# Second half of the next pair's y loaded at the 19th unit of the passes, not the 24th, into other rooms

## The chip, the cores and the metric

One core of a Trainium2 chip runs the whole program. The metric is device time in microseconds, as the median of several runs. Five engines work side by side, each in the order of its own instructions: TensorE (PE in the profile; PEld is its weight load), VectorE (DVE), ScalarE (ACT), GpSimd (POOL) and SyncE (SP), which here issues most DMA transfers. 16 DMA engines move the data; SP's transfers are queue q1 in the profile, GpSimd's are q0.

## The reference

```python
def _attn_ref(q, k, v, mem_k, mem_v):          # chunks of 32 queries, 16 + 32 + 8 keys and 8 memory keys
    ...
        scores = scale * np.matmul(q_c, k_full.transpose(0, 1, 3, 2))
        a = np.exp(scores - np.max(scores, axis=-1, keepdims=True))
        out[:, :, c_start:c_end] = np.matmul(a / (np.sum(a, axis=-1, keepdims=True) + 1e-09), v_full)

def _moe_ref(x, w_in, w_out):
    h = x @ w_in
    return (np.maximum(h, 0.0) + np.log1p(np.exp(-np.abs(h)))) @ w_out

def _moe2_ref(x, w_in, w_out, alpha):
    h = x @ w_in
    return (np.maximum(h, 0.0) + alpha * np.minimum(h, 0.0)) @ w_out

x = attn_out.transpose(0, 2, 1, 3).reshape(B * S, H * D)      # 3072 tokens x 512
return _moe2_ref(_moe_ref(x, ...), ...)                       # 512 -> 2048 -> 512, twice; all float32
```

## The kernel before, in words

Attention and the first MLP fill the first part of the program, under an order that a planner in the kernel works out; the change touches nothing of it. Their result y, 512 rows by 3072 tokens, lies in device memory (`y_dram`), in six blocks of 512 tokens.

The second MLP takes the blocks in three pairs, p = 0, 1, 2. For a pair it multiplies 2x2 blocked matrices with seven products in place of eight (Winograd's form of Strassen's method), so that it works on sums and differences of blocks. Each float32 operand is split in a high and a low part, and each product is three matmuls. A pair has two stages of 336 matmuls:

- **Quads** (`quad`, eight of them): x operands (`xop`) times `win`. The results G[0] to G[3] lie in tiles `gb`.
- **Passes** (`second`): seven passes of eight *units*, n = 0 to 55. A unit takes one G tile, splits it into a `g` tile (a cast on ScalarE for the high part, a subtraction on VectorE for the low part) and has six matmuls with an eighth of `wout`. The `g` of a unit is made some three units ahead. The 14 `wout` loads of 1 MiB, called weights 0 to 13 below, each serve four units: weight j serves units 4j to 4j + 3. Six accumulating DMAs from GpSimd (`gb<-gb`, 1 MiB each) add G tiles to each other between passes.

While `second(p)` runs, `prepare(p + 1)` puts the preparation of the next pair's x operands between its units: at a unit given by a table, it issues loads, subtractions and splits. The work is in two halves, h = 0 and 1, each with 128 of the 256 rows of a block row. For each half four tiles of 128 x 512, 256 KB each, are loaded (`load_y`): B11, T1 (which comes as B12), B21 and B22; they are called the four y quarters of that half below. Three subtractions on VectorE follow (`sum_y`): the first difference T3 = T1 - B11, the second difference T2 = B22 - T3, and T1 = B22 - T1. `sum_last` makes T4 = B21 - T2. Then each of the seven is split into `xop` (`split_y`: a ScalarE cast and a VectorE subtraction). Each of these steps stands in program order between the `g` steps of its engine; nothing overtakes on an engine. The last pair prepares nothing.

Rooms come from pools of fixed count: `w` (16 rooms: `wout`, `win`, three `gb` rooms a half, five of the seven `xop`), `raw` (4 rooms: some `g`, results `c`, T2 and T3 as `yt`), `yraw` (4 rooms of one tile: the y quarters and T4), `word` (3 rooms: temporary results). A load into a used room waits until its last reader is done. SP issues in order too, so a load that waits holds back all that follow. SP's DMAs share eight semaphores in turn, so a DMA also waits until the one issued eight before it has landed. The results `c` are transposed and stored from inside the passes (`flip`).

Of the kernel before, what the change touches and what calls it, by code (L numbers as in the profile page):

```python
# [7 lines left out]
F32 = mybir.dt.float32  # L8
# [8 lines left out]
P = 128  # L17
# [30 lines left out]
N2 = 512  # L48
# [20 lines left out]
B11, B21, B22, T1, T2, T3, T4 = range(7)  # L69
# [162 lines left out]
def attention_mlp_mlp_kernel(ctx: ExitStack, tc, qk, v, w1, w2, consts, out):  # L232
    nc = tc.nc

    def room_pool(name, bufs, space=None):
        kw = {} if space is None else {"space": space}
        return tc.tile_pool(name=name, bufs=bufs, **kw)

    cpool = ctx.enter_context(room_pool("const", 1))
    wpool = ctx.enter_context(room_pool("w", NF))  # L240
    tpool = ctx.enter_context(room_pool("t", 1))
    gpool = ctx.enter_context(room_pool("g", 2))
    xpool = ctx.enter_context(room_pool("x", 4))
    rpool = ctx.enter_context(room_pool("raw", 4))
# [513 lines left out]
    def store_last(d, b, m):  # L758
        sp.dma_start(out=y_dram[(2 * d + m) * P:(2 * d + m + 1) * P, (LP + b) * N2:(LP + b + 1) * N2], in_=c_1[d, b][:, m, :])

    y_raw, x_op, w_in, w_out, slots, G, g2 = {}, {}, {}, {}, {}, {}, {}

    def switch_pools():
# [4 lines left out]
    def raw_y(name):  # L768
        return late["x"].tile([P, N2], F32, tag="yraw", name=name, bufs=4)

    def load_y(p, h):

        for key, kc, b in ((B11, h, 0), (T1, h, 1), (B21, h + 2, 0), (B22, h + 2, 1)):
            t = y_raw[p, h, key] = raw_y("yraw")
            tok = (2 * p + b) * N2
            sp.dma_start(out=t, in_=y_dram[kc * P:(kc + 1) * P, tok:tok + N2])

    def sum_y(p, h, n):
        if n == 0:
            two = rpool.tile([P, 2, N2], F32, tag="raw", name="yt")  # L780
            y_raw[p, h, T2], y_raw[p, h, T3] = (two[:, e] for e in range(2))
        to, a, b = ((T3, T1, B11), (T2, B22, T3), (T1, B22, T1))[n]
        dve.tensor_tensor(out=y_raw[p, h, to], in0=y_raw[p, h, a], in1=y_raw[p, h, b], op=ALU.subtract)
        if n == 2:
            y_raw[p, h, T1], y_raw[p, h, T3] = y_raw[p, h, T3], y_raw[p, h, T1]

    def sum_last(p, h):
        t4 = y_raw[p, h, T4] = raw_y("yt")
        dve.tensor_tensor(out=t4, in0=y_raw[p, h, B21], in1=y_raw[p, h, T2], op=ALU.subtract)

    def split_y(p, h, k):
        high_y(p, h, k)
        low_y(p, h, k)
# [266 lines left out]
    def prepare(p):  # L1060

        if p >= NPAIRS:
            return {}
        todo = {}
        for h in range(2):
            load, add, last, split = ((1, 8, 12, (11, 13, 15, 17, 19, 21, 23)), (24, 30, 34, (33, 36, 38, 44, 45, 47, 48)))[h]
            todo.setdefault(load, []).append(lambda h=h: load_y(p, h))
            for k in range(3):
                todo[add + k] = [lambda h=h, k=k: sum_y(p, h, k)]
            for n, k in zip(split, (B11, B21, B22, T1, T2, T3, T4)):  # L1070
                todo[n] = [lambda h=h, k=k: split_y(p, h, k)]
            todo[last] = [lambda h=h: sum_last(p, h)]
        return todo

    def pairs(between):
        for p in range(NPAIRS):
            for q in range(NQ):
                quad(p, q, between, ready if q == NQ - 1 else lambda n: None)
                between = lambda: None
            between = second(p, prepare(p + 1))  # L1080
# [5 lines left out]
    last = len(steps) - 1  # L1086
# [6 lines left out]
    def schedule(when):  # L1093
# [256 lines left out]
        for h in range(2):  # L1350
            due = end + 10 + 26 * h
            dma(("yl", h), 1.6, 2.9, due, lambda h=h: load_y(0, h), ["switch", ("out", last + 7)], ["y"] * 4)
            add(("ysum", h), "DVE", 2.1, due + 8, lambda h=h: [sum_y(0, h, n) for n in range(3)], [("yl", h)], ["raw"])
            order_y = (B11, B21, B22, T1, T2, T3, T4)
            for n, k in enumerate(order_y):
                after = [("ysum", h)] + ([("yo", h, order_y[n - 1])] if n else []) + ([("yo", 0, k)] if h else [("h", last)] if k < 2 else [("sf", 3)])
                if k == B21:
                    add(("y4", h), "DVE", 0.7, due + 10, lambda h=h: sum_last(0, h), after, ["y"])
                    after = [("y4", h)]
                add(("yo", h, k), "ACT", 0.62, due + 10 + 2 * n - O["yo"], lambda h=h, k=k: high_y(0, h, k), after, ["w"] if not h and k > 1 else [])  # L1360
                add(("yd", h, k), "DVE", 0.72, due + 11 + 2 * n - O["yo"], lambda h=h, k=k: low_y(0, h, k), [("yo", h, k)], [], [] if k == T1 else ["raw"] if k == T2 else ["y"])
# [92 lines left out]
```

## Time and profile before

| what | us |
|---|---|
| median of 3 runs (lowest, highest) | 1091.04 (1090.74, 1093.18) |
| the profiled execution, whole | 1093.45 |
| its span, first to last instruction | 1091.7 |
| TensorE busy in it | 1058.8 (97%) |
| VectorE busy | 793.2 (73%) |
| ScalarE busy | 561.3 (51%) |
| mean granted TensorE clock | 0.995 |

The profile is of one execution, and all times of rows are microseconds from its span's start. Matmuls are pipelined, so a row's length for one matmul is more than its share of the stretch. A bracket such as [6.54 <-DVE g L80] is the time that the engine stood idle before the row and what ended it. All engines' calls go through one helper, so every row has line L80; rows are told apart by their tiles, as out<-in.

### The profile page before, as it was taken

The page shows a single profiled execution, that of the slowest core. Times are in us where ns is not written, and L with a number is a line of the kernel's source. Part 1 is how long each engine was busy: PE and PEld are TensorE (multiplying, and loading weights), DVE is VectorE, ACT ScalarE, POOL GpSimd, SP SyncE. Part 2 cuts the span into 40 slices and gives each one's busy share as a digit, 9 for nine tenths or more (in the row PEclk, how much of TensorE's full clock was granted, in tenths as well). Part 3 has the DMA queues.
Part 4 walks back from the last instruction along what each step waited for, and adds up shares of the span by engine and source line. Part 5 has one row for each costly group of instructions (what it writes and reads, how often), then busy time and mean ns, then how long its engine had stood idle before and what let it go on. Part 6 is the DMA issues. An engine that isn't in the chain of part 4 may idle for free.

```text
span 1091.7 us, 18778 instructions
## 1 busy us (share of the span) xinstructions
PE 1058.8 (97%) x7229; PEld 861.2 (79%) x7233; DVE 793.2 (73%) x1318; ACT 561.3 (51%) x958; POOL 161.8 (15%) x177
## 2 busy tenths in 40 slices
PE   7799999999999999999999999997999999999998
PEld 4578888787878888888878888885888887888886
DVE  5789995775766788876377666767666759566976
ACT  4564454454543555553354555653455655456643
POOL 0110110422222442235410000000000000000000
PEclk9999999999999999999999999998999999999999
DMA  9886688868657576865999645997775998856804
GB/s 224 210 211 207 173 236 277 225 209 234 199 186 230 177 256 195 259 204 171 336 330 284 226 157 174 328 298 209 185 280 180 339 299 233 244 206 258 370 1 78
DMA packets 171705, 248.25 MB, mean 227 GB/s; under 512 B 79328, under 2 KB 123488, under 8 KB 162400
## 3 DMA queue, kind: packets, MB, share of 16 engines
q1 hardware_dynamic: 166736, 225.95, 63.6%
q0 software_dynamic: 4608, 20.97, 9.8%
q8 instruction: 57, 0.93, 0.4%
q14 instruction: 32, 0.26, 0.1%
q10 hardware_dynamic: 272, 0.13, 0.0%
HBM read 169.42 MB, written 60.82 MB: 211 GB/s over the span
## 4 chain that ended last, share of the span: by engine, by line
PE 86%; DMA 6%; DVE 5%; ACT 1%; issue 1%; SPq 0%; POOL 0%; DVEq 0%; ACTq 0%
PE ps_q L80 45%; PE ps_hh L80 22%; PE ps_o L80 15%; PE ps_a L80 3%; DMA yraw<-y_dram 3%; DMA raw<-in_w_dram 2%; DVE word L80 1%; DVE g L80 1%; ACT v L80 1%; DVE sm L80 1%; DVE x L80 0%; DVE pt L80 0%; DMA qk<-in_qk_dram 0%; ACT g L80 0%; DVE nm L80 0%
## 5 line engine op out<-in xcount | busy, mean ns | idle before, releaser
L80 PE MATMUL ps_q<-g,wout 128*128 128x512 f32 x1344 | 311.3, 392 | 9.2 <-DVE g L80 8.7
L80 PEld LDWEIGHTS ps_q<-g,wout 128*128 128x128 f32 x1344 | 252.8, 189 | 66.5 <-DVE g L80 14.0
L80 PE MATMUL ps_hh<-x,wsplit 128*128 128x512 f32 x1152 | 277.5, 393 | 1.7 <-DVE x L80 1.5
L80 PEld LDWEIGHTS ps_hh<-x,wsplit 128*128 128x128 f32 x1152 | 215.2, 188 | 48.5 <-DVE x L80 2.1
L80 PE MATMUL ps_q<-xop,win 128*128 128x512 f32 x1008 | 229.0, 389 | 0.0
L80 PEld LDWEIGHTS ps_q<-xop,win 128*128 128x128 f32 x1008 | 189.2, 188 | 39.2
L80 ACT CAST g<-gb 128x512 fp32r<-128x512 f32 x224 | 133.0, 621 | 129.2 <-PE ps_q L80 107.4
L80 DVE TENSOR_TENSOR g<-gb,g 128x512 fp32r<-128x512 f32 x224 | 154.0, 700 | 61.5 <-ACT g L80 59.6
L80 PE MATMUL ps_o<-g,wsplit 128*128 128x512 f32 x768 | 188.2, 393 | 2.9 <-issue 1.6
L80 PEld LDWEIGHTS ps_o<-g,wsplit 128*128 128x128 f32 x768 | 142.4, 188 | 33.7 <-DVE g L80 2.1
L80 ACT ACTIVATE ta<-ps_hh 128x512 f32<-128x512 f32 x88 | 52.6, 598 | 123.4 <-PE ps_hh L80 123.1
L80 DVE SCALAR_TENSOR_TENSOR word<-raw,word 128x512 int32<-128x512 int32 x128 | 94.4, 738 | 2.6
L80 DVE TENSOR_TENSOR g<-ta,g 128x512 fp32r<-128x512 f32 x64 | 53.5, 836 | 39.6 <-ACT g L80 39.5
L80 ACT ACTIVATE tp<-gb 128x512 f32<-128x512 f32 x48 | 30.4, 633 | 90.7 <-DVE gb L80 90.7
L80 DVE SCALAR_TENSOR_TENSOR gb<-gb,tp 128x512 f32<-128x512 f32 x48 | 33.2, 692 | 45.5 <-ACT tp L80 45.5
L80 POOL TENSOR_TENSOR wst<-word,wst 128x512 fp32r<-128x512 f32 (+2 forms) x40 | 44.6, 1120 | 143.5 <-ACT wst L80 128.2
L80 POOL DMA_DIRECT2D gb<-gb x16 | 13.8, 862 | 331.4 <-DVE g L80 193.8
L80 DVE TENSOR_SCALAR word<-word 128x512 f32<-128x512 f32 (+1 forms) x128 | 57.4, 456 | 1.6
L80 ACT ACT_TABLE_LOAD x38 | 48.8, 1283 | 13.5 <-DVE nm L80 10.8
L80 ACT CAST g<-ta 128x512 fp32r<-128x512 f32 x64 | 39.8, 622 | 21.8 <-PE ps_o L80 21.0
L80 POOL TENSOR_TENSOR wst<-wst 128x1024 fp32r<-128x1024 f32 x16 | 42.0, 2623 | 20.7 <-ACT wst L80 18.6
L80 DVE TENSOR_SCALAR word<-raw 128x512 int32<-128x512 int32 x64 | 34.9, 545 | 11.3 <-DMA raw<-in_w_dram 11.1
(95 smaller groups left out, 920.4 us busy)
## 6 DMA issues: line engine op xcount, KB each, us to landing
wout<-out_ops SPq DMA_DIRECT2D x42, 1024.0 KB
raw<-in_w_dram SPq DMA_DIRECT2D x64, 512.0 KB
win<-in_ops SPq DMA_DIRECT2D x24, 1024.0 KB
win<-in_ops SPq DMA_DIRECT2D x24, 768.0 KB
gb<-gb POOLq DMA_DIRECT2D x16, 1024.0 KB, 13.8
wout<-outs SPq DMA_DIRECT2D x14, 1024.0 KB
in_ops<-wst SPq DMA_DIRECT2D x24, 512.0 KB
outs<-wst SPq DMA_DIRECT2D x16, 512.0 KB
```

The source lines that it names most:

```text
L80: i = getattr(self.engine, name)(*args, **kw)
```

## The change

Four things change, all for pairs 1 and 2 (that is, in `second(0)` and `second(1)`):

- The second half's four loads are issued at unit 19 instead of 24, its three subtractions stand at units 26 to 28 instead of 30 to 32, T4 at 30 instead of 34, the splits of B11 and B21 at 29 and 31 instead of 33 and 36. The other splits stay.
- T2 and T3 of the first half leave the `raw` pool and take half of a room of the `w` pool (`side`, four tiles).
- The other half of that room takes B11 and T1 of the second half. Of the four `yraw` rooms the second half's B21 and B22 take two, its T2 and T3 the other two.
- The second half's T4 takes a `word` room.

```diff
+    side = {}
...
-            t = y_raw[p, h, key] = raw_y("yraw")
+            t = y_raw[p, h, key] = side[p][:, 2 + (key == T1), :] if p and h and key in (B11, T1) else raw_y("yraw")
...
         if n == 0:
-            two = rpool.tile([P, 2, N2], F32, tag="raw", name="yt")
-            y_raw[p, h, T2], y_raw[p, h, T3] = (two[:, e] for e in range(2))
+            if p == 0:
+                two = rpool.tile([P, 2, N2], F32, tag="raw", name="yt")
+            elif h == 0:
+                two = side[p] = wpool.tile([P, 4, N2], F32, tag="w", name="yt")
+            y_raw[p, h, T2], y_raw[p, h, T3] = (raw_y("yt") if p and h else two[:, e] for e in range(2))
...
-        t4 = y_raw[p, h, T4] = raw_y("yt")
+        t4 = y_raw[p, h, T4] = tpool.tile([P, N2], F32, tag="word", name="yt", bufs=3) if p and h else raw_y("yt")
...
-            load, add, last, split = ((1, 8, 12, (11, 13, 15, 17, 19, 21, 23)), (24, 30, 34, (33, 36, 38, 44, 45, 47, 48)))[h]
+            load, add, last, split = ((1, 8, 12, (11, 13, 15, 17, 19, 21, 23)), (19, 26, 30, (29, 31, 38, 44, 45, 47, 48)))[h]
```

The order on SP in the first pair's passes, before: weights 7, 8 and 9, the second half's B11, T1, B21 and B22, then weights 10 and 11. A bracket names the semaphores that the row waits for: DMAHW for landings of SP's DMAs, DMASW for GpSimd's, DVE or PE for the last reader of the room.

```order
L80 DMA wout_7332<-out_ops_91 128x2048 [waits DMAHW2_49]
L80 DMA wout_7380<-out_ops_91 128x2048 [waits DMAHW3_49,PE_49]
L80 DMA wout_7425<-out_ops_91 128x2048 [waits DMAHW4_49,PE_49]
L80 DMA yraw_7444<-y_dram_88 128x512 [waits DMAHW5_49,DVE_49]
L80 DMA yraw_7446<-y_dram_88 128x512 [waits DMAHW6_49,DVE_49]
L80 DMA yraw_7448<-y_dram_88 128x512 [waits DMAHW7_49,DVE_49]
L80 DMA yraw_7450<-y_dram_88 128x512 [waits DMAHW0_49,DVE_49]
L80 DMA wout_7476<-out_ops_91 128x2048 [waits DMAHW1_49,PE_49]
L80 DMA wout_7517<-out_ops_91 128x2048 [waits DMAHW2_49,DMASW5_49]
```

The same place on SP now: weights 7 and 8, the four quarters (B11 and T1 as `yt_7256`), then weights 9 and 10.

```order
L80 DMA wout_7332<-out_ops_91 128x2048 [waits DMAHW2_49,PE_49]
L80 DMA wout_7380<-out_ops_91 128x2048 [waits DMAHW3_49,PE_49]
L80 DMA yt_7256<-y_dram_88 128x512 [waits DMAHW4_49]
L80 DMA yt_7256<-y_dram_88 128x512 [waits DMAHW5_49]
L80 DMA yraw_7391<-y_dram_88 128x512 [waits DMAHW6_49,DVE_49]
L80 DMA yraw_7393<-y_dram_88 128x512 [waits DMAHW7_49,DVE_49]
L80 DMA wout_7431<-out_ops_91 128x2048 [waits DMAHW0_49,DMASW4_49,DVE_49]
L80 DMA wout_7477<-out_ops_91 128x2048 [waits DMAHW1_49,DMASW5_49,DVE_49]
```

The quarters moved ahead of weight 9; two of them wait for no reader, the other two for VectorE. Weight 7 now waits for a room, and weight 9 waits for a `gb` room.

The order on VectorE in the first pair's passes, before, from the low part of `g` 26 on (one `g` row is one unit); `yt_7509` is the first and then the second difference.

```order
L80 TENSOR_TENSOR g_7441<-gb_6531,g_7441 128x512
L80 TENSOR_TENSOR g_7458<-gb_6531,g_7458 128x512
L80 TENSOR_TENSOR g_7467<-gb_6839,g_7467 128x512
L80 TENSOR_TENSOR g_7478<-gb_6839,g_7478 128x512
L80 TENSOR_TENSOR g_7487<-gb_6839,g_7487 128x512
L80 TENSOR_TENSOR g_7496<-gb_6839,g_7496 128x512
L80 TENSOR_TENSOR g_7506<-gb_6530,g_7506 128x512
L80 TENSOR_TENSOR yt_7509<-yraw_7446,yraw_7444 128x512
L80 TENSOR_TENSOR g_7519<-gb_6530,g_7519 128x512
L80 TENSOR_TENSOR yt_7509<-yraw_7450,yt_7509 128x512
L80 TENSOR_TENSOR g_7531<-gb_6530,g_7531 128x512
L80 TENSOR_TENSOR u2_7534<-ps_q_7433,u2_7352 128x512
```

The same place on VectorE now, from `g` 26 on; `yt_7469` is the first difference, `yt_7468` the second, `yt_7514` is T4.

```order
L80 TENSOR_TENSOR g_7447<-gb_6531,g_7447 128x512
L80 TENSOR_TENSOR g_7456<-gb_6531,g_7456 128x512
L80 TENSOR_TENSOR g_7465<-gb_6839,g_7465 128x512
L80 TENSOR_TENSOR yt_7469<-yt_7256 128x512
L80 TENSOR_TENSOR g_7479<-gb_6839,g_7479 128x512
L80 TENSOR_TENSOR yt_7468<-yraw_7393,yt_7469 128x512
L80 TENSOR_TENSOR g_7489<-gb_6839,g_7489 128x512
L80 TENSOR_TENSOR yt_7256<-yraw_7393,yt_7256 128x512
L80 TENSOR_TENSOR g_7499<-gb_6839,g_7499 128x512
L80 TENSOR_TENSOR xop_7291<-yt_7256,xop_7291 128x512
L80 TENSOR_TENSOR g_7511<-gb_6530,g_7511 128x512
L80 TENSOR_TENSOR yt_7514<-yraw_7391,yt_7468 128x512
```

The first difference moved from behind `g` 32 to behind `g` 28, and from there on one other step follows each `g`.

The order on ScalarE near units 49 to 51 of those passes, before; `c_7738` is the third result (negated A12 product), and the eight landings that a row waits for are the first result's stores.

```order
L80 CAST g_7703<-gb_6531 128x512 [waits DMASW0_49,DVE_49,PE_49]
L80 CAST g_7722<-gb_6531 128x512 [waits DMAHW4_49,DMAHW5_49,DMAHW3_49,DMAHW6_49,DMAHW2_49,DMAHW7_49,DMAHW1_49,DMAHW0_49]
L80 CAST xop_7407<-yraw_7446 128x512
L80 CAST g_7735<-gb_6531 128x512 [waits DVE_49,PE_49]
L80 ACTIVATE c_7738<-ps_q_7243 128x512
```

The same place on ScalarE now.

```order
L80 CAST g_7702<-gb_6531 128x512 [waits DMASW0_49,DVE_49,PE_49]
L80 CAST g_7721<-gb_6531 128x512
L80 CAST xop_7413<-yt_7256 128x512
L80 CAST g_7734<-gb_6531 128x512 [waits DVE_49,PE_49]
L80 ACTIVATE c_7737<-ps_q_7243 128x512 [waits DMAHW4_49,DMAHW5_49,DMAHW3_49,DMAHW6_49,DMAHW2_49,DMAHW7_49,DMAHW1_49,DMAHW0_49]
```

The wait for the first result's stores moved from a `g` cast to the third result's copy, three instructions later.

## Rows read from the trace of the kernel before

**Rows 1.** Stages by stretch: us, busy (count) by engine, clock, DMA share, GB/s.
```profile
692.36:778.00 85.64, 79.04 (x338) 64.48 (x337) 61.40 (x98) 43.94 (x79) 5.16 (x6) 0.96 0.90 258
...
854.15:933.71 79.56, 77.74 (x338) 62.58 (x336) 61.13 (x98) 43.96 (x79) 5.16 (x6) 1.00 0.96 276
...
1009.87:1086.05 76.18, 76.18 (x337) 62.97 (x336) 62.40 (x100) 36.79 (x65) 0.00 (x0) 1.00 0.46 154
```
**Rows 2.** Chain of waits of the whole span: start, length, what.
```profile
725.08 19.39 DMA yraw<-y_dram
745.17 0.70 DVE g L80
745.91 138.35 PE ps_q L80 x599
...
886.86 13.87 DMA yraw<-y_dram
```
**Rows 3.** Timeline of TensorE, second MLP: start, length, what, [idle before <-releaser].
```profile
692.36 47.01 PE L80 MATMUL ps_q<-g,wout 128*128 128x512 f32 x205
745.91 32.25 PE L80 MATMUL ps_q<-g,wout 128*128 128x512 f32 x131 [6.54 <-DVE g L80]
...
902.17 5.26 PE L80 MATMUL ps_q<-g,wout 128*128 128x512 f32 x18 [1.38 <-DVE g L80]
```
**Rows 4.** A stretch behind the first pair's stall, columns as in rows 1.
```profile
745.90:750.70 4.80, 4.79 (x11) 3.80 (x12) 4.80 (x9) 0.00 (x0) 0.00 (x0) 0.50 1.01 406
```
**Rows 5.** Timeline of VectorE, first pair's passes, 725 to 748.
```profile
727.24 1.29 DVE L80 TENSOR_TENSOR g<-gb,g 128x512 fp32r<-128x512 f32 x2 [0.67 <-ACT g L80]
729.96 0.69 DVE L80 TENSOR_TENSOR g<-gb,g 128x512 fp32r<-128x512 f32 x1 [1.43 <-ACT g L80]
...
736.36 0.69 DVE L80 TENSOR_TENSOR yt<-yraw 128x512 f32<-128x512 f32 x1 [1.63 <-DMA yraw<-y_dram]
...
744.56 0.69 DVE L80 TENSOR_TENSOR yt<-yraw,yt 128x512 f32<-128x512 f32 x1 [6.91 <-DMA yraw<-y_dram]
```
**Rows 6.** Timeline of SP's DMA issues, first pair's passes.
```profile
698.02 0.32 SPq L80 DMA_DIRECT2D wout<-out_ops  x1
...
714.34 0.32 SPq L80 DMA_DIRECT2D wout<-out_ops  x1
714.75 10.65 SPq L80 DMA_DIRECT2D yraw<-y_dram  x4
725.50 0.42 SPq L80 DMA_DIRECT2D wout<-out_ops  x1
...
757.33 4.27 SPq L80 DMA_DIRECT2D out_dram<-c  x8
```
**Rows 7.** Timeline of VectorE, 711 to 716: splits of the first half's B21 and B22.
```profile
711.53 0.69 DVE L80 TENSOR_TENSOR xop<-yraw,xop 128x512 fp32r<-128x512 f32 x1
...
713.49 0.68 DVE L80 TENSOR_TENSOR xop<-yraw,xop 128x512 fp32r<-128x512 f32 x1
```
**Rows 8.** DMA queues, 695 to 728.5: queue, packets, MB, share of 16 engines.
```profile
q1 hardware_dynamic: 789, 5.71, 42.8%
```
**Rows 9.** DMA queues, 728.5 to 732.
```profile
q1 hardware_dynamic: 547, 1.36, 98.2%
q0 software_dynamic: 11, 0.02, 3.5%
```
**Rows 10.** DMA queues, 733 to 745.
```profile
q0 software_dynamic: 234, 1.77, 70.7%
q1 hardware_dynamic: 250, 1.55, 32.4%
```
**Rows 11.** DMA queues, second pair's passes, 857 to 890.
```profile
q1 hardware_dynamic: 761, 5.58, 42.1%
```
**Rows 12.** DMA queues, second pair's passes, 890 to 894.
```profile
q1 hardware_dynamic: 643, 1.59, 100.3%
```
**Rows 13.** Timeline of VectorE, second pair's passes: `g` 29.
```profile
891.74 0.69 DVE L80 TENSOR_TENSOR g<-gb,g 128x512 fp32r<-128x512 f32 x1 [1.43 <-ACT g L80]
```

## The prediction

> **What bounds the kernel now.** I read first the stages of the second MLP, as stretches between the changes of TensorE's operands [rows 1]. Each pair of token blocks has 336 matmuls of quads and 336 of passes. The last pair's passes, which prepare no further pair, take 76.18 us. The same 336 matmuls take 85.64 us in the first pair and 79.56 us in the second. So 9.46 and 3.38 us, 12.84 in all, are lost in the two passes that load and split the next pair's y. The change touches nothing else, so 12.84 us is the most that it can give.
>
> Then the chain of waits [rows 2]: inside the passes it leaves TensorE twice, for two y loads (from issue to landing 19.39 and 13.87 us), and comes back through one `g` step on VectorE. In the first pair TensorE stands idle for 6.54 us, until 745.91 [rows 3]; then for 4.80 us the granted clock is 0.50, which is 1.2 GHz of the two levels, and 11 matmuls start where 2.4 GHz would fit 21 [rows 4]: about 2.3 us more. 6.54 + 2.3 is 8.8 of the 9.46. The second pair's clock stays at 1.00 over its whole stage [rows 1].
>
> Last, VectorE, which runs strictly in order [rows 5]. At 736.36 it forms the first difference (T1 - B11 of the second half) after 1.63 us idle for a y landing, and at 744.56 the second difference after 6.91 us idle for B22. Each `g` behind them is a unit's right operand. A unit is 76.18/56 = 1.36 us, and unit n starts at 692.36 + 1.36n until the stall.
>
> **The loads.** SP issues weight 8 at 698.02 and weight 9 at 714.34 (weights 0 to 13 are a pair's 1 MiB loads), then the four y quarters from 714.75 on, over 10.65 us, because the last two wait for VectorE to free rooms; the last goes out only at 725.08 [rows 2, 6]. In the changed order B11 and T1 need no room of VectorE's, and B21 and B22 take the rooms that the first half's B21 and B22 leave after the splits at 711.53 and 713.49 [rows 7]. All four can be issued by about 714.5, 10.6 us before the last now, and ahead of weight 9.
>
> What this does to landings is read from the queue's bytes. From 695 (my estimate of where weight 4 starts; 1 us more or less is 0.15 MB, 0.4 us at the end) SP's queue, q1, moves 5.71 MB until 728.5 [rows 8], and 1.36 MB in the next 3.5 us, 0.39 per us, while the accumulations (q0) are nearly silent [rows 9]. Five weights, 4 to 8, are 5.24 MB; y is 1.05 MB. So in the new order the average engine has T1 (5.77 MB) at 728.7 and all of y (6.29 MB) at 730.0. Landing is the slowest of 16 engines. By the old order T1 ends 6.82 MB, average 731.3, and was used at 736.36: 5.1 us late. B22 ends 7.34 MB, average some 733.3, and landed at 744.47: 11 us late. This lateness is made by the fifth accumulation: from 733 to 745 q1 has 250 records and q0 234 [rows 10], about one turn for one, 12 x 16/234 = 0.82 us each, and a quarter of y has 8 rows of 2 KB per engine, up to 6.6 us. T1's last 736.3 - 732.5 = 3.8 us are about 4.6 such rows; the slow engine was thus at T1's fourth row when the average one was 0.54 MB further, 1.4 us at 0.39. With that lag, and up to 1 us for rows that still share turns with the fourth accumulation, I put T1 at 731.0 and B22 at 732.5, before the accumulation returns. The bounds are the average, 730.0, and the old order's lateness, 735.1 or 741.
>
> The Trainium skill ("DMA: Bandwidth & Descriptors", Queues, rings and completion order) says an engine drains a whole packet of several descriptors, typically 9 to 17, before it turns to the next queue. By it a quarter's 8 rows would leave in one turn and B22 would land near the average time, 730 to 731.4, and the sum below would lose 0.4 us of its residue. The records of [rows 10], 250 to 234, say one row a turn, so I keep the later time.
>
> **VectorE's part.** The moved steps are as many as before: three subtractions, one more, seven splits; nothing is added on any engine. But the first difference now stands behind `g` 28 and not `g` 32, four units (5.44 us) earlier. `g` 27 and 28 end at 728.5 [rows 5]; TensorE needs `g` 29 at 731.8, and its low part one matmul later, 732.0. With T1 at 731.0, subtraction (0.60 to the next start) and `g` 29 (0.69) end at 732.3: 0.3 us lost. With B22 at 732.5 the second difference and `g` 30 end at 733.8, needed at 733.4 + 0.3: 0.1 us. Afterwards the new order has one other step per `g`, 2 x 0.60 = 1.2 us per unit, under 1.36; the old one had two beside some `g`, 1.8 us, which I take for the second pair's loss beyond its 1.38 us idle [rows 3].
>
> **What moves behind it.** Weight 8 must now wait for a room, since the y side room has taken the spare one: weight 7, which waited for no room, does now. Its issue moves to between 698 and 714.3. The queue then still holds weights 5 to 7 (5.71 MB are not through before 728.5), so this costs nothing while that backlog is there; without it, up to the 5 to 16 us that it is later. Weight 9 is needed at unit 36 (741.3) and weight 10 at unit 40 (746.8). Sixteen turns per engine from 732.5 on, beside the accumulations, at 0.82 are 13.1 us, so 745.6; from 735 it is 748.1. I take 0.3 us, bounds 0 and 1.3. ScalarE's wait for the first result's stores stands three instructions later than before; behind it are casts of later units. The stores, issued at 757.33 after the stall [rows 6], come about 8 us earlier, but each waits for the landing eight issues back, the last for weight 13; counting bytes at 0.39 that is near 754, plus some 2 us, and A12's last unit ends at 692.4 + 48 x 1.36 + 1 = 758.6. No cost.
>
> **Second pair.** q1 moves 5.58 MB from 857 to 890 [rows 11], then 1.59 MB in 4 us [rows 12]. All of y is through on average at 890 + 0.71/0.40 = 891.8, with the same lag 893.2; T1 at 892. `g` 29 came at 891.74 [rows 13], and TensorE needs it at 854.15 + 39.4 + 0.2 = 893.8: no loss; B22 costs 0 to 0.3.
>
> **Sum.** First pair 9.46 - (0.4 + 0.3 + 0.3 for what I can't see) = 8.46. Second pair 3.38 - 0.3 = 3.08. Together 11.5 us. The profiled execution took 1093.45 us, span 1091.7, so 1081.9 by it; the runs' median is 1091.04, from which I count: 1079.5. The bounds of y's landing give 12.8 at the best (1078.2) and some 5 us less at 735 with 2.4 us of weight 10 and unseen waits (1084 to 1086).
>
> **Rivals.** (a) Part of the stall stays: the slowest engine is caught by the fifth accumulation before B22's rows are through. For: in the old order exactly this cost 11 us. Against: 2.3 us lie between 730.0 and 732.3. B22 at 735 to 737 leaves 3 to 5 us in the first pair, and the clock stays up: 1083 to 1088, taken at 1085.
>
> (b) The change doesn't do what it says, or the loads take each other's place: SP is in order, so if the y loads stand behind weight 8 waiting for its room, or weights 9 and 10 come late by what y gained, TensorE waits at unit 36 or 40 instead. The Trainium skill ("DMA: Bandwidth & Descriptors", Issuing engines are not separate DMA queues) has all queues on the same 16 engines, so that nothing is gained but order; the rows agree. By the bytes, though, weight 10 comes where it came before, and it was needed 9 us later than now; 9 us lost there gives 1089 to 1092.
>
> (c) Slower: VectorE stops earlier. The first difference stands 5.44 us earlier in its order, so any landing less than 5.44 us earlier than now makes TensorE wait longer than now. That point is 739.0 in the first pair and 900.73 - 5.44 = 895.3 in the second (landing by the chain, 886.86 + 13.87 [rows 2]). With B22 served at the old pace, 742 and 898.5, the loss grows by 3 and 3.2 us, and the second pair may then fall to the lower clock as the first did, 2.3 us: 1091.04 + 8.5 = 1099.5. Against it: 895.3 is 2 us, 739.0 6.5 us behind my times.
>
> **Chances.** Forecast 0.70 (own range 1078 to 1082.5), (a) 0.17, (b) 0.07, (c) 0.06. Differences under 0.2%, 2.2 us, this measurement can't tell from none. Faster: 0.70 + 0.17 + a third of (b), 0.89; same 0.05; slower 0.06. The range 1077.5 to 1087.0 takes the forecast and nearly all of (a).
>
> **What would show it.** Right: passes of the first two pairs near 77.2 and 76.5 us; the clock at 1.00; all four y loads issued by 715; no VectorE idle over 1.5 us before a `yt`; y gone from the chain. Wrong: TensorE idle at unit 29 or 30 with a `yt` behind a y load (a or c), or idle at unit 36 or 40 with no VectorE wait (b).

## The result, and the profile after

The changed kernel takes 1081.21 us (median of 4 runs, 1080.35 to 1082.83), the kernel before, run beside it, 1091.24 (4 runs, 1090.74 to 1093.18): ratio 0.9907, 95% interval 0.9889 to 0.9924. The forecast was 1079.5, the range 1077.5 to 1087.0. Runs over 1.5% above the fastest of the same kernel count as slow and are left out of every figure here (five of the 29 of the kernel before that ran beside e5 to e8).

The profiled execution took 1080.35 us, span 1078.6. TensorE's timeline, to be laid beside [rows 3] (start, length, what, [idle before <-releaser]):

```profile
691.66 76.76 PE L80 MATMUL ps_q<-g,wout 128*128 128x512 f32 x336
768.26 76.32 PE L80 MATMUL ps_q<-xop,win 128*128 128x512 f32 x336
844.42 76.34 PE L80 MATMUL ps_q<-g,wout 128*128 128x512 f32 x336
920.60 76.32 PE L80 MATMUL ps_q<-xop,win 128*128 128x512 f32 x336
```

Each stage is one row now; the idle brackets of 6.54 and 1.38 us are gone. The two passes as stretches, with the columns of [rows 1]:

```profile
691.66:768.26 76.60, 76.50 (x337) 62.94 (x336) 61.44 (x98) 43.84 (x79) 5.16 (x6) 1.00 0.99 286
844.42:920.60 76.18, 76.18 (x337) 63.04 (x336) 61.81 (x98) 43.87 (x79) 5.15 (x6) 1.00 1.00 288
```

Over the floor of 76.18 the first pair loses 0.42 us (9.46 before), the second nothing (3.38 before). The granted clock is 1.00 in both; the 4.8 us at 0.50 [rows 4] went with the stall that preceded them. VectorE, ScalarE and GpSimd run 98, 79 and 6 instructions in a pair's passes, as before; nothing was saved but waiting. The DMA share of the first pair rose from 0.90 to 0.99: the same bytes in fewer microseconds.

SP's issues in the first pair's passes, to be laid beside [rows 6]:

```profile
687.94 15.14 SPq L80 DMA_DIRECT2D wout<-out_ops  x5
703.13 1.03 SPq L80 DMA_DIRECT2D yt<-y_dram  x2
711.54 2.28 SPq L80 DMA_DIRECT2D yraw<-y_dram  x2
714.11 22.03 SPq L80 DMA_DIRECT2D wout<-out_ops  x5
...
747.34 8.07 SPq L80 DMA_DIRECT2D out_dram<-c  x8
```

B11 and T1 go out behind weight 8, B21 and B22 by 713.8, and only then weight 9. VectorE there, to be laid beside [rows 5]:

```profile
726.54 1.30 DVE L80 TENSOR_TENSOR g<-gb,g 128x512 fp32r<-128x512 f32 x2 [0.67 <-ACT g L80]
730.27 0.69 DVE L80 TENSOR_TENSOR yt<-yt 128x512 f32<-128x512 f32 x1 [2.43 <-DMA yt<-y_dram]
730.88 0.68 DVE L80 TENSOR_TENSOR g<-gb,g 128x512 fp32r<-128x512 f32 x1
731.60 0.69 DVE L80 TENSOR_TENSOR yt<-yraw,yt 128x512 f32<-128x512 f32 x1
732.21 0.69 DVE L80 TENSOR_TENSOR g<-gb,g 128x512 fp32r<-128x512 f32 x1
```

The first difference still waits for T1, 2.43 us, but the second finds B22 there. TensorE needed the `g` between them at about 731.2 and got it at 731.6: that is the 0.42. The chain of waits therefore still passes through one y load (start, length, what):

```profile
703.66 26.51 DMA yt<-y_dram
...
730.27 0.69 DVE yt L80
730.96 0.61 DVE g L80
...
731.62 48.60 PE ps_q L80 x213
```

It is T1, 26.51 us from issue to landing. Before, T1 went out 23.0 us after the passes' start and landed at 43.9 (by the trace's landing events), 20.9 us; now it goes out at 12.0 and lands at 38.5. It waits longer in the queue and comes earlier. The length of a transfer on the chain is not itself the loss.

### The profile page after: what moved, and what is told of

It reads as the page before. It is cut to its first block, busy times and chain, and to the rows that moved or that the text cites. A ratio compares the mean times of both kernels' runs of the same rounds, so it can differ in the third digit from the quotient of the medians.

```text
span 1078.6 us, 18773 instructions
## 1 busy us (share of the span) xinstructions
PE 1054.8 (98%) x7233; PEld 860.5 (80%) x7233; DVE 793.1 (74%) x1318; ACT 561.2 (52%) x958; POOL 160.5 (15%) x177
## 4 chain that ended last, share of the span: by engine, by line
PE 89%; DMA 5%; DVE 3%; SPq 1%; issue 1%; ACT 0%; POOL 0%; DVEq 0%; ACTq 0%
PE ps_q L80 47%; PE ps_hh L80 23%; PE ps_o L80 15%; PE ps_a L80 3%; DMA yt<-y_dram 2%; DMA qk<-in_qk_dram 1%; SPq L80 1%; DMA v<-in_v_dram 1%; DVE g L80 1%; DVE word L80 0%; DMA raw<-in_w_dram 0%; DVE pt L80 0%; PE ps_x L80 0%; DVE sm L80 0%; PE ps_s L80 0%
## 5 line engine op out<-in xcount | busy, mean ns | idle before, releaser
L80 PE MATMUL ps_q<-g,wout 128*128 128x512 f32 x1344 | 307.2, 390 | 0.9 <-DVE g L80 0.8
L80 PEld LDWEIGHTS ps_q<-xop,win 128*128 128x128 f32 x1008 | 189.2, 188 | 39.3
L80 DVE TENSOR_TENSOR g<-ta,g 128x512 fp32r<-128x512 f32 x64 | 53.2, 830 | 40.0 <-ACT g L80 39.7
L80 ACT ACT_TABLE_LOAD x38 | 48.8, 1283 | 13.8 <-DVE nm L80 11.1
L80 ACT CAST g<-ta 128x512 fp32r<-128x512 f32 x64 | 39.8, 622 | 22.2 <-PE ps_o L80 21.4
```

The source lines that it names most:

```text
L80: i = getattr(self.engine, name)(*args, **kw)
```

## The experiments

Ratios of e1 to e4 are against the kernel before at 1092.17 us (25 runs, 1084.49 to 1099.69), of e5 to e8 against 1089.23 (24 runs, 1080.77 to 1096.21). The ratio is not the quotient of the two medians; the two differ by up to 0.3%. The table has the profiled executions: when T1 and B22 of the second half landed (the last of a transfer's 16 landing events in the trace, counted from the first matmul of the passes), and what the passes took over 76.18 us; first pair / second pair.

| kernel | T1 landed | B22 landed | lost, us | median us | ratio, 95% interval |
|---|---|---|---|---|---|
| before | 43.9 / 39.8 | 52.1 / 46.6 | 9.46 / 3.38 | 1091.24 | |
| after | 38.5 / 37.1 | 39.8 / 38.4 | 0.42 / 0.00 | 1081.21 | 0.991 (0.989 to 0.992) |
| e1_rooms | 40.1 / 39.4 | 46.9 / 42.5 | 3.68 / 0.37 | 1088.40 | 0.998 (0.994 to 1.002) |
| e2_loads | 37.4 / 37.1 | 38.7 / 38.4 | 0.37 / 0.34 | 1082.53 | 0.989 (0.984 to 0.994) |
| e3_steps | 40.0 / 39.9 | 46.2 / 46.1 | 8.39 / 8.25 | 1098.64 | 1.004 (1.001 to 1.007) |
| e4_sums | 39.5 / 39.8 | 43.8 / 46.6 | 0.59 / 3.43 | 1091.45 | 0.998 (0.995 to 1.002) |
| e5_before_again | 41.8 / 39.6 | 51.8 / 44.5 | 9.14 / 1.27 | 1091.90 | 0.9995 (0.996 to 1.003) |
| e6_nine_behind | 37.4 / 37.5 | 38.7 / 38.8 | 0.35 / 0.35 | 1081.85 | 0.992 (0.988 to 0.995) |
| e7_no_last_sums | 40.7 / 40.4 | 42.0 / 41.7 | 0.34 / 0.37 | 1081.72 | 0.992 (0.989 to 0.994) |
| e8_after_again | 38.0 / 37.3 | 39.4 / 38.7 | 0.02 / 0.02 | 1081.42 | 0.994 (0.990 to 0.998) |

**e1_rooms: the change's rooms, the table of before.** From the changed kernel:

```diff
-(19, 26, 30, (29, 31, 38, 44, 45, 47, 48))
+(24, 30, 34, (33, 36, 38, 44, 45, 47, 48))
```

> The change's rooms, but the table of before: loads at unit 24, subtractions at 30 to 32. No load of the second half waits for VectorE any more, and all four are issued by some 718, 7 us before the last one before, but behind weight 9. Theory A (place in SP's queue and the turns with the fifth accumulation set the landing): y still ends 7.34 MB into the queue, the slow engines still meet the accumulation, B22 lands near 744 in the first pair, TensorE still stands some 6 us there; median 1089 to 1092. Theory B (the wait of the last two loads for rooms was what made them late): B22 lands 7 us or more earlier, before it is needed; median 1081 to 1083.

SP issued the four loads together, but behind weight 9:

```profile
718.44 1.01 SPq L80 DMA_DIRECT2D yt<-y_dram  x2
719.49 1.01 SPq L80 DMA_DIRECT2D yraw<-y_dram  x2
725.78 13.90 SPq L80 DMA_DIRECT2D wout<-out_ops  x4
```

TensorE stopped at the same place as before, for less:

```profile
695.63 46.65 PE L80 MATMUL ps_q<-g,wout 128*128 128x512 f32 x205
743.93 3.45 PE L80 MATMUL ps_q<-g,wout 128*128 128x512 f32 x12 [1.66 <-DVE g L80]
```

The last load was issued 24.4 us after the passes' start, where before it was 32.7, and its first landing event came at 39.3 us, where before it was 39.4. Eight us of earlier issue brought nothing at the front of the transfer. Neither theory's times came: B22 landed 46.9 us after the passes' start, between A's 52 and B's 45 or less, and the median lies between theirs. Whether the shorter stall is the rooms' doing one execution can't tell, and the median's difference is inside its interval.

**e2_loads: the change's rooms and loads, subtractions and splits where they were.** From the changed kernel:

```diff
-(19, 26, 30, (29, 31, 38, 44, 45, 47, 48))
+(19, 30, 34, (33, 36, 38, 44, 45, 47, 48))
```

> The change with loads at unit 19, but the subtractions, T4 and the first two splits at the units of before (30 to 36). Landing as in the changed kernel, y 5 us early. Theory A: no idle of VectorE for y; what may stay is VectorE's crowding at units 33 to 39 (11 other steps beside 7 g steps, 18 x 0.605 = 10.9 us in 9.5): up to 1.4 us in each pair, so 1081 to 1084. Theory C (the second pair's 2 us beyond its idle 1.38 is crowding, and moving the subtractions is what gave them back in both pairs): 3 to 5 us more than the changed kernel, 1084 to 1086.

All of the gain is there. Of VectorE's places only 0.34 to 0.37 us a pair is left, lost between units 36 and 44, where results and y steps stand together. The changed kernel, which differs from e2 by those places alone, loses nothing between these units in any of its four profiled pairs (its 0.42 is the wait for T1, at unit 29). So crowding costs about 0.35 us, not the 2.0 that the prediction gave it in the second pair.

**e3_steps: the change's rooms, subtractions and splits, loads where they were.** From the changed kernel:

```diff
-(19, 26, 30, (29, 31, 38, 44, 45, 47, 48))
+(24, 26, 30, (29, 31, 38, 44, 45, 47, 48))
```

> The change's rooms and its subtractions at units 26 to 28, but the loads at unit 24, behind weight 9. Theory A: y lands as before (B22 near 744 and 901) and is needed 5.4 us earlier, so TensorE waits some 12 us in the first pair and 6 to 7 in the second, each with a fall of the clock: 1098 to 1106, slower than before. Theory B (issue time decides): all four are issued by 718, 7 us before the last one before; landing near 737 and 894, median 1083 to 1090.

VectorE in the first pair:

```profile
733.93 0.69 DVE L80 TENSOR_TENSOR yt<-yt 128x512 f32<-128x512 f32 x1 [3.96 <-DMA yt<-y_dram]
734.54 0.68 DVE L80 TENSOR_TENSOR g<-gb,g 128x512 fp32r<-128x512 f32 x1
740.13 0.69 DVE L80 TENSOR_TENSOR yt<-yraw,yt 128x512 f32<-128x512 f32 x1 [4.90 <-DMA yraw<-y_dram]
```

and TensorE in both pairs:

```profile
735.28 1.67 PE L80 MATMUL ps_q<-g,wout 128*128 128x512 f32 x6 [1.63 <-DVE g L80]
741.48 37.05 PE L80 MATMUL ps_q<-g,wout 128*128 128x512 f32 x155 [4.52 <-DVE g L80]
...
895.95 1.67 PE L80 MATMUL ps_q<-g,wout 128*128 128x512 f32 x6 [1.54 <-DVE g L80]
902.13 37.04 PE L80 MATMUL ps_q<-g,wout 128*128 128x512 f32 x155 [4.51 <-DVE g L80]
```

This is rival (c) itself: landings close to those of e1, needed four units earlier, and two stops a pair of 6.1 us together, after which the granted clock is 0.50 for some 3.4 us. It is slower than before by 0.4% (0.1 to 0.7). It also shows what one accumulation does: the sixth goes out at 49.1 us after the passes' start here, behind B22's landing at 46.2, so the fifth alone made B22 6 us late (the ninth of its 16 landings came at 40.2).

**e4_sums: the fifth and sixth accumulation later in the program.** From the kernel before:

```diff
-30: (0, 1, 2), 35: (1, 1, 2)}
+34: (0, 1, 2), 38: (1, 1, 2)}
```

> The kernel before with the fifth and sixth accumulating DMA of a pair asked for at units 34 and 38 instead of 30 and 35; no other edit, y loads and their order as before. Theory A (the turns with the fifth accumulation made the last quarters late): B22 lands near 734 in the first pair and 895 in the second, TensorE's idle time there goes or falls under 1 us; median 1081 to 1085. Theory B (rooms, issue at 725): B22 stays late, median 1089 to 1092. If the accumulations come too late for the last pass, TensorE waits at units 48 or 52 instead.

The edit moved nothing: GpSimd has no other work there and sends an accumulation when its tile's last reader is done, 35.87 us after the passes' start, 35.86 before. So it doesn't test the accumulation. In what is sent when, it is the kernel before once more, and that is what it shows: no stall in the first pair (0.59), the old one in the second (3.43).

**e5_before_again: the kernel before, unchanged.**

> The kernel before, run again unchanged, to see how far its stall differs between executions. Theory: the y loads' place behind weight 9 leaves their last rows to the beginning of the fifth accumulation, and how many rows are left then depends on how far the slowest DMA engine lags in that execution; so the losses over 76.18 us scatter, between 0.5 and 9.5 us in a pair, with B22's landing anywhere from 43 to 52 us after the passes' start; median 1091. Rival: the stall has a fixed length, 9.46 and 3.38 us as profiled, within 0.5 us.

TensorE, first and second pair:

```profile
693.53 46.65 PE L80 MATMUL ps_q<-g,wout 128*128 128x512 f32 x205
746.80 32.21 PE L80 MATMUL ps_q<-g,wout 128*128 128x512 f32 x131 [6.62 <-DVE g L80]
...
855.01 77.61 PE L80 MATMUL ps_q<-g,wout 128*128 128x512 f32 x336
```

The two executions of the kernel before lost 12.84 and 10.41 us, and e4, with the same work at the same times, 4.02: the stall has no fixed length, as the theory said. The two of the kernel before alone differ in the second pair (3.38 and 1.27); in the first they agree within 0.3 us, as the rival said, and the 4.80 us behind that stop again have the clock at 0.50.

**e6_nine_behind: weight 9 behind the four y loads, nothing else.** From the kernel before:

```diff
-                if n // 4 + 4 < 14:
+                if n // 4 + 4 < 14 and (n != 23 or p == NPAIRS - 1):
                     load_w_out(14 * p + n // 4 + 4)
...
             for piece in todo.get(n, ()):
                 piece()
+            if n == 24 and p < NPAIRS - 1:
+                load_w_out(14 * p + 9)
```

> The kernel before with one thing moved: weight 9 is issued behind the four y loads of the second half, at unit 24 instead of 23. Rooms, subtractions and the y loads' own issue times stay as before (the last still near 32.7 us after the passes' start). Theory of the place in the queue: the 2.7 us of weight 9's bytes no longer lie ahead, B22 lands near 39 to 40.5 us after the passes' start, before the fifth accumulation, TensorE does not stop, each pair loses under 1 us: median 1081 to 1083, as the changed kernel. Rival, the time of issue decides (the change wins by issuing the last load 10.9 us earlier): the issue is not earlier, so the stall stays and the median is about 1091. Second rival: weight 9 itself, issued 11 us later, is late at unit 36 (49.0 us after the passes' start): TensorE stops there, with no VectorE wait.

SP, TensorE and VectorE of it:

```profile
715.42 13.16 SPq L80 DMA_DIRECT2D yraw<-y_dram  x4
728.68 5.48 SPq L80 DMA_DIRECT2D wout<-out_ops  x5
```

```profile
695.56 76.70 PE L80 MATMUL ps_q<-g,wout 128*128 128x512 f32 x336
...
848.28 76.69 PE L80 MATMUL ps_q<-g,wout 128*128 128x512 f32 x336
```

```profile
737.83 0.69 DVE L80 TENSOR_TENSOR yt<-yraw 128x512 f32<-128x512 f32 x1
738.58 0.69 DVE L80 TENSOR_TENSOR g<-gb,g 128x512 fp32r<-128x512 f32 x1
739.19 0.69 DVE L80 TENSOR_TENSOR yt<-yraw,yt 128x512 f32<-128x512 f32 x1
```

The last y load still goes out at 32.7 us after the passes' start, as before (B11 and T1 2.5 and 1.2 us earlier). Yet it lands 13.4 us earlier than in the profile of before, the stall is gone in both pairs, and so is the change's whole gain reached, with no new room and no moved subtraction. The time of issue is refuted as the cause; the place in SP's queue is shown as it. Weight 9, issued 11 us later, was not missed: no wait stands before unit 36.

**e7_no_last_sums: the kernel before without its fifth and sixth accumulation** (the products that use that sum are then of other numbers):

```diff
-15: (0, 0, 1), 19: (1, 0, 1), 30: (0, 1, 2), 35: (1, 1, 2)}
+15: (0, 0, 1), 19: (1, 0, 1)}
```

> The kernel before without its fifth and sixth accumulations (G[1] += G[2] is left out in both halves, so the products that use that sum are of other numbers; the instructions of the other engines are the same). Theory: the lateness of the last y rows is made by the fifth accumulation, so B22 lands by 42 us after the passes' start in both pairs and each pair loses under 1 us: about 1081. Rival: the slowest engine is late on SP's own queue alone, whatever the accumulations do: B22 lands at 46 to 52 and the losses stay at 3 to 9 us a pair, 1088 to 1092.

The same order on SP as before, y behind weight 9, and no stall. The queues from 732 to 744, first of the changed kernel, where the fifth accumulation runs, then of e7 (queue, packets, MB, share of 16 engines):

```profile
q0 software_dynamic: 225, 1.71, 68.5%
q1 hardware_dynamic: 224, 1.66, 34.4%
```

```profile
q1 hardware_dynamic: 582, 4.04, 81.0%
```

Beside the accumulation SP's queue gets one record for each of the accumulation's, and 1.66 MB where it moved 4.04 without it and then had nothing left in the last 2 us. A y row that has not been served when the accumulation begins pays for that; without it B22 is through at 42 us even behind weight 9. The run leaves out two accumulations and can't tell the fifth from the sixth; e3 shows the fifth alone.

**e8_after_again: the changed kernel again.**

> The changed kernel run again, to see whether its small loss is an accident of one execution. Theory of the place in the queue: B22 has been ahead of the fifth accumulation's begin by several us in any execution, so both pairs lose under 1 us again; median 1081 to 1083. Rival: the changed kernel too has executions in which the slowest engine is caught, and a pair then loses 3 us or more.

Lost: 0.02 us in each pair. The first difference waited 1.94 us on VectorE and TensorE noticed nothing. The eight runs lie between 1078.29 and 1084.38, 6 us apart, where 24 of the kernel before are 15 us apart (more runs, so not a like comparison).

## Why the prediction was right, and where it was off

**The bound, right, for that execution.** 12.84 us were there to be had, and 12.42 of them came back between the two profiles. The medians moved 10.0 us. The difference is the one step of the sum that failed: "the runs' median is 1091.04, from which I count: 1079.5" takes the stall of one execution for that of the median run. The stall scatters (e4, e5), and the profiled execution, at 1093.45 us, lies above the median of 1091.24 and above all the runs beside it (highest 1093.18). The passes' start scatters too, by 5 us over all profiles; how much of the missing 2.4 us is the stall's scatter and how much the start's, no run shows. The stage itself was better than forecast (0.42 lost, 1.3 expected), the starting point worse.

**The landings, right.** From the passes' start T1 was forecast at 38.6 and B22 at 40.1 us in the first pair, measured 38.5 and 39.8; in the second 37.9 and 39.1, measured 37.1 and 38.4. The fifth accumulation's first records come between 39 and 40 us after the passes' start in each of six profiles looked at (before, after, e1, e4, e5, e6; both pairs). What is through by then is safe: e6 has it so by order, e7 by taking the last two accumulations away. The reason in the prediction ("This lateness is made by the fifth accumulation") is thereby shown where B22 lands by 46.6 us (the second pair of before, e3). In the first pair it is only part of it: the fifth had landed at 48.0 us and B22 came at 52.1, so its last rows fell beside the sixth, which went out at 40.6. The Trainium skill's rule weighed there ("DMA: Bandwidth & Descriptors", Queues, rings and completion order: a whole packet of several descriptors before the next queue has its turn) is not borne out as counted in records: 225 to 224 here, 232 to 240 in 12 us of e5's stall. The records name no engine, but in the second pair of before only ten y rows start after 40.0 us, most of them 0.70 us apart (41.27, 41.97, 42.67 and so on to 45.48), then one after 0.10. An accumulation's record takes 0.63 us there and a y row 0.08, which fits one accumulation row between two y rows on one late engine; the prediction took 0.82 us a turn.

**VectorE's part, right in its sum, wrong in its signs.** 0.4 us were forecast, 0.42 measured. But "no VectorE idle over 1.5 us before a `yt`" contradicted the prediction's own numbers: `g` 28 done by 728.5 and T1 at 731.0 make 2.5 us of idle, and 2.43 were seen. VectorE runs ahead of TensorE there and may wait about 2 us for nothing (1.94 in e8). For the same reason y stayed on the chain in one execution and left it in another (e8).

**Crowding, wrong.** "The old one had two beside some `g`, 1.8 us" was taken for the 2.0 us that the second pair lost beyond its idle 1.38. In [rows 3] that pair needs 5.4 us for the 18 matmuls behind the stop, 4.1 at the floor; in the same stretch VectorE is never idle:

```profile
902.10:907.50 5.40, 4.97 (x18) 3.15 (x18) 5.40 (x11) 1.42 (x3) 0.00 (x0) 1.00 1.02 276
```

It is catching up on steps held back by the late B22. With y in time the same places cost 0.35 us (e2, e6, e7). That this part of the sum came out right was luck: the loss, too, went with the stall.

**What moves behind it, right.** Weight 8 went out at 11.1 us after the passes' start instead of 5.7 and landed at 36.4 instead of 36.2. Weight 10 was forecast to land at 53.2, landed at 53.3, and cost nothing (0.3 allowed). The first result's stores came 10 us earlier (747.34) without a cost that shows.

**Rivals.** (a) and (b) did not happen. (c) is real and is what the earlier subtractions alone do (e3): 8.4 and 8.3 us lost in place of 9.5 and 3.4. The change would have been slower had its loads stayed behind weight 9.

Open: why the slowest DMA engine lags more in one execution than in the next. The medians of e5 to e8 can't tell e6 from the changed kernel (1081.85 and 1081.42); no version beat it, and with 0.02 us lost a pair these stages hold nothing more to win.

## What to carry to other kernels

Where a queue has a backlog, as here, a load's landing is set by what stands ahead of it in the order, not by when it is issued (e1, e6): before giving it an earlier slot and more rooms, try to swap it with a large load that is needed later. A wait that ends on the slowest of 16 DMA engines, beside another queue that has just begun, can scatter from run to run (0.6 to 9.5 us in the first pair here); profile the kernel more than once before taking its length for the gain. Move a consumer earlier only together with its load.

## What was not expected of the hardware

- A stall of 0.6 us in e4 and of 9.5 us in before, both in the first pair, with the same work sent at the same times. The landing events of one 1 MiB weight lay 6.2 us apart in that pair of before (weight 7: 22.57 to 28.78), 3.9 in e4.
- The changed kernel's weight 7 was just as ragged (6.3 us, first pair) without harm, because the slowest engine's last y row was through at 39.8 us, as the fifth accumulation began. The kernel before has the average engine through at 40.4 (the 9th of B22's 16 landings), so each row that an engine lags behind can meet the accumulation.
- The first passes began anywhere from 690.59 to 695.63 us in these ten profiles, without relation to the kernel: 5 us of scatter come from the earlier part of the program, which no edit touched.
